# Turning the last 64 rows of four tiles apart, with their twin columns partly on GpSimd and the first copy on VectorE

## The chip, the cores and the metric

The kernel runs on one NeuronCore of a Trainium2 chip (trn2). The metric is device time in microseconds (us) of one execution. The ratios below are the mean time of one kernel's fast runs over the mean of the other's fast runs of the same rounds, so they are not quite the ratios of the medians quoted beside them.

Names used throughout: TensorE is PE in the profile, its weight loads PEld, VectorE DVE, ScalarE ACT, GpSimd POOL.

## The reference, cut to what matters

```python
xn = layernorm(x)                       # x: 2048 tokens x 448
s  = linear_attention(xn, wqkv, wo)     # q, k, v = xn @ wqkv; 16 heads of 28
h  = relu(xn @ w1 + b1) ** 2            # 448 -> 1792
g  = silu(h @ w2 + b2)
return x + s * g
```

The products with `wqkv` and `w1` take `xn` transposed, channels on partitions. 448 channels are three chunks of 128 and a rest of 64. A matmul over the rest has 64 rows (`64*128` in the profile, where a full chunk has `128*128`), and the kernel runs such matmuls in pairs, one on rows 0 to 63 and one on rows 64 to 127. In the kernel before the first pair, of 512 columns each, starts at 8.366 and 8.370 us and the next pair at 8.592: two of them in 0.226 us, where one matmul of 128 rows and 512 columns steps by 0.216. For the pairs the kernel keeps the last 64 channels on partitions 0 to 63 and again on 64 to 127: they are written twice before the transpose ("twin columns").

## The kernel before: the opening

The tokens are 16 tiles of 128. Tiles 4 to 15 are transposed by DMA, much later. Tiles 0 to 3, the opening, are transposed by TensorE into PSUM and copied to `xT`. The kernel lists operations by engine; a list scheduler orders VectorE, ScalarE and GpSimd, with a fixed order in the opening. TensorE's instructions stay in the order of the program.

```python
# (cut) statistics on VectorE, rstd = exp(-0.5*ln(var+eps)) on ScalarE, then on VectorE:
#   ln_norm: xn[:, si, 0:256], xn[:, si, 256:384] (tiles 0, 1) or xn[:, si, 0:384] (tiles 2, 3)
def ln_last(si):     # last 64 columns and their twins in one instruction
    x = x_tok[:, si, 384:448]
    x = bass.AP(tensor=x.tensor, offset=x.offset, ap=[x.ap[0], [0, 2], x.ap[1]])
    return add("dve", lambda e, _: e.tensor_scalar(
        out=xn[:, si, 384:512].rearrange("p (i c) -> p i c", i=2), in0=x, scalar1=mv[:, si, 0:1],
        scalar2=rstd[:, si : si + 1], op0=ALU.subtract, op1=ALU.mult), ...)

def pe_transpose(si, part, eng):   # transposes of one bank, then one copy to xT
    b = Buf("T")
    chunks = range(4) if part is None else (2 * part, 2 * part + 1)
    # (cut) one e.transpose for each chunk; a copy on `eng` of all chunks
    # (tile 0, part 0: two copies of one chunk each)

# rests(): the 64-row matmuls that complete a unit, two units at once
# phase((a, ks), (c, ks)): unit a on rows 0-63 beside unit c on rows 64-127
# pe_four(a, b, c, d): phase((a,K4),(c,K4)); phase((b,K4),(d,K4)); phase((c,K3),(a,K3)); phase((d,K3),(b,K3))
#   with K4 = (3, 0, 1, 2), K3 = (0, 1, 2): the rest (chunk 3) comes first
warm(8, wide=True)                 # 8 dummy matmuls of 512 columns
turn(0, 0, "act"); turn(0, 1, "act"); turn(1, 0, "act")
mains(k0, (0,)); mains(k0, (1,)); mains(k0, (2,))       # K of tile 0, 512 columns each
turn(1, 1, "act")
mains(k1, (0, 1)); h_mains(0, (0, 1)); mains(k1, (2,))  # K of tile 1; H of tiles 0 and 1
# (cut) transpose of b1
h_mains(0, (2,)); h_mains(1); h_mains(2)
head["xT2"] = pe_transpose(2, None, "act")
h_mains(3)
head["xT3"] = pe_transpose(3, None, "dve")
rests(k0, k1); rests(first[0], first[2]); rests(first[1], first[3])
pe_four(*second)                   # H of tiles 2 and 3
```

I call the second group of K matmuls (`mains(k1, (0, 1))`) "the second K group" and the first phase of the last line "the tile 2/3 phase".

Of the kernel before, what the change touches and what calls it, by code (L numbers as in the profile page):

```python
# [9 lines left out]
P = 128  # L10
# [45 lines left out]
class Program:  # L56
# [8 lines left out]
    def add(self, eng, emit, reads=(), writes=(), dur=0.2, alts=(), nbytes=0):  # L65
        op = Op(eng, emit, reads, writes, dur, alts, nbytes)
        for t in op.reads:
            w = self.writer.get(t)
            if w is not None:
                op.raw.add(w)  # L70
            self.readers.setdefault(t, []).append(op)
        for t in op.writes:
            w = self.writer.get(t)
            if w is not None and w is not op:
                op.deps.add(w)
            for r in self.readers.get(t, ()):
                if r is not op:
                    op.deps.add(r)
            self.writer[t] = op
            self.readers[t] = [r for r in self.readers.get(t, ()) if r is op]  # L80
        op.raw.discard(op)
        op.deps |= op.raw
        for d in op.deps:
            d.succ.append(op)
        self.ops.append(op)
        return op
# [203 lines left out]
def bass_recurrent_scan__linear_attn_block__dense_activation_squared_relu__prompt_kernel(  # L290
# [4 lines left out]
    with ExitStack() as es:  # L295
        sb = lambda name, shape, dtype: es.enter_context(nc.sbuf_tensor(name, shape, dtype))
        bf, f32 = dt.bfloat16, dt.float32
        pr = Program()
        add = pr.add

        ident = sb("ident", [P, P], bf)
# [7 lines left out]
        xn = sb("xn", [P, NT, 512], bf)  # L309
        xT = sb("xT", [P, 4, S], bf)  # L310
# [8 lines left out]
        mv = sb("mv", [P, NT, 2], f32)  # L319
        vep = sb("vep", [P, NT], f32)  # L320
        rstd = sb("rstd", [P, NT], f32)
# [23 lines left out]
        ps = lambda b: pbank[b.bank]  # L345
# [94 lines left out]
        wnames = lambda name: [(name, i) for i in range(4 if name == "w1a" else 3)]  # L440
# [53 lines left out]
            )  # L494

        xn_of = lambda si: [("xn", si, 0), ("xn", si, 1)] if si < 2 else [("xn", si)]
        xT_of = lambda si: [("xT", si, j) for j in ("a", 0, 1)[si > 0 :]] if si < 4 else [("xT", si)]

        def ln_twin(lo, hi, eng="dve"):

# [7 lines left out]
        def ln_last(si):  # L508

            x = x_tok[:, si, 384:448]  # L510
            x = bass.AP(tensor=x.tensor, offset=x.offset, ap=[x.ap[0], [0, 2], x.ap[1]])
            return add(
                "dve",
                lambda e, _: e.tensor_scalar(
                    out=xn[:, si, 384:512].rearrange("p (i c) -> p i c", i=2), in0=x, scalar1=mv[:, si, 0:1],
                    scalar2=rstd[:, si : si + 1], op0=ALU.subtract, op1=ALU.mult,
                ),
                [("x", si), ("mv", si), ("rstd", si)], [("xd", si)], 0.18,
            )

        def pe_transpose(si, part, eng):


            b = Buf("T")
            chunks = range(4) if part is None else (2 * part, 2 * part + 1)
            for i, c in enumerate(chunks):
                reads = xn_of(si)[c // 2 :][:1] or xn_of(si) if c < 3 else [("xd", si)]
                add(
                    "pe",
                    lambda e, _, i=i, c=c: e.transpose(  # L530
                        ps(b)[:, i * 64 : (i + 1) * 64].bitcast(bf), xn[:, si, c * P : (c + 1) * P], ident[:, :]
                    ),
                    reads + ["ident"] + ([b] if i else []), [b], 0.1,
                )
            def ev(e, _, lo=0, n=len(chunks)):
                src = ps(b)[:, lo * 64 : (lo + n) * 64].bitcast(bf).rearrange("p (c k) -> p c k", c=n)
                dst = xT[:, chunks[0] + lo : chunks[0] + lo + n, si * P : (si + 1) * P]
                if eng == "dve":
                    return e.tensor_copy(dst, src)
                return e.activation(out=dst, in_=src, func=AF.Copy)  # L540

            names = [("xT", si, j) for j in ((0, 1) if part is None else (part,))]
            if (si, part) == (0, 0):
                head["xT00a"] = add(eng, lambda e, x: ev(e, x, 0, 1), [b], [("xT", 0, "a")], 0.25)
                return add(eng, lambda e, x: ev(e, x, 1, 1), [b], names, 0.25)
            return add(eng, ev, [b], names, (0.42 if eng == "dve" else 0.6) if part is None else 0.25 if eng == "dve" else 0.35)

        def dma_transpose(si):
            op = add(
# [10 lines left out]
        def phase(lo, hi):  # L560


            todo = []
            order = [(i / len(ks), h, u, k) for h, (u, ks) in enumerate((lo, hi)) for i, k in enumerate(ks)]
            for _i, h, u, k in sorted(order, key=lambda o: o[:2]):
                todo.append((u, h, k, u.count == 0, u.count == u.steps - 1))
                u.count += 1

            def f(e, _):
                last = None  # L570
                for u, h, k, start, stop in todo:
                    last = u.mm(e, h, k, start, stop)
                return last

            reads, us = [], [u for u, ks in (lo, hi) if ks]
            for u in us:
                reads += [r for r in u.reads if r not in reads]
            dur = max(len(ks) * MM(u.n) for u, ks in (lo, hi) if ks)
            op = add("pe", f, reads + [u.bank for u in us if u.op], [u.bank for u in us], dur)
            for h, (u, ks) in enumerate((lo, hi)):  # L580
                if ks:
                    if u.op and u.half != h:
                        op.sync.add(u.op)
                    u.op, u.half = op, h
            for u in us[::-1]:
                if u.count == u.steps:
                    u.out()

        K4, K3 = (3, 0, 1, 2), (0, 1, 2)

        def pe_four(a, b, c, d):

            phase((a, K4), (c, K4))
            phase((b, K4), (d, K4))
            phase((c, K3), (a, K3))
            phase((d, K3), (b, K3))

        def mains(u, ks=K3, reads=None):


            def f(e, _):
                for k in ks:
                    last = u.mm(e, 2, k, k == 0, False)
                return last

            reads = u.reads if reads is None else reads
            add("pe", f, reads + ([u.bank] if ks[0] else []), [u.bank], len(ks) * MM(u.n))
# [440 lines left out]
        head = {}  # L1048
# [21 lines left out]
        k0, k1 = kk(0), kk(1)  # L1070
        first = [hh(0, fi, 0) for fi in range(4)]
        second = [hh(0, fi, 1, first[fi].bank) for fi in range(4)]

        def turn(si, part, eng):
            head[f"xT{si}{part}"] = pe_transpose(si, part, eng)

        def h_mains(fi, ks=K3):
            xs = xT_of(0) + xT_of(1)
            mains(first[fi], ks, [x for x in xs if 2 in ks or x[2] != 1] + [("w1a", fi // 2 * 3)])

        turn(0, 0, "act")
        turn(0, 1, "act")
        turn(1, 0, "act")
        mains(k0, (0,), [("xT", 0, "a")] + wnames("wk")[:1])
        mains(k0, (1,), [("xT", 0, 0)])
        mains(k0, (2,), [("xT", 0, 1)])
        turn(1, 1, "act")
        mains(k1, (0, 1), [("xT", 1, 0)] + wnames("wk")[:1])
        h_mains(0, (0, 1))
        mains(k1, (2,), [("xT", 1, 1)])  # L1090
        bb = Buf("B1")
        b1v = lambda: ps(bb)[:, 0 : P // 2].bitcast(bf)
        add("pe", lambda e, _: e.transpose(b1v(), b1r[:, :], ident[:, :]), ["b1r", "ident"], [bb], 0.1)
# [1 line left out]
            "act", lambda e, _: e.activation(out=b1f[:, :], in_=b1v()[:, 0:NF], func=AF.Copy), [bb], ["b1f"], 0.2  # L1095
        )
        h_mains(0, (2,))
        h_mains(1)
        h_mains(2)
        head["xT2"] = pe_transpose(2, None, "act")  # L1100
        h_mains(3)
        head["xT3"] = pe_transpose(3, None, "dve")
        n = len(pr.ops)
        rests(k0, k1)
        k0.out()
# [2 lines left out]
        rests(first[0], first[2])  # L1108
        rests(first[1], first[3])
        for eng, names in (  # L1110
            ("dve", "st0 mv0 st1 mv1 xn00 xn01 xd0 xn10 xn11 xd1 st2 mv2 st3 mv3 xd2 xn2 xd3 xn3 xT3"),
            ("act", "ln0 ex0 ln1 ex1 xT00a xT00 xT01 xT10 xT11 ln2 ex2 ln3 ex3 b1 xT2"),
        ):
            ops = [head[n] for n in names.split()]
            for i, op in enumerate(ops):
                op.after = ops[:i]
                op.prio = -100 + i
        for op in early:
            op.after = [head["xT3" if op.eng == "dve" else "xT2"]]
        pe_four(*second)  # L1120

        def quads(g, what):

# [15 lines left out]
        for g, (first, second) in enumerate(streams):  # L1139
            if g + 1 < NG:  # L1140
                n = len(pr.ops)
# [106 lines left out]
```

## Time and profile before

| what | before |
|---|---|
| time, median of 3 | 141.26 us (141.19 to 141.45) |
| TensorE busy | 136.5 of 139.5 us (98%) |
| first transpose | 4.190 us |
| first K matmul | 5.030 us |
| second K group | 5.789 us |
| tile 2/3 phase | 8.954 us |

The page of the kernel before, its engine line and the head of its chain that ended last:

```profile
PE 136.5 (98%) x1255; PEld 68.0 (49%) x1255; DVE 92.2 (66%) x226; ACT 78.0 (56%) x152; POOL 25.0 (18%) x33
...
PE 95%; DVE 2%; DMA 2%; issue 0%; DVEq 0%
```

TensorE bounds the kernel. The next view of the kernel before is the busy time by stretch: us in the stretch, then busy us of each engine.

```profile
core 0: us, PE busy (x) PEld busy (x) DVE busy (x) ACT busy (x) POOL busy (x), PEclk, DMA share, GB/s
...
9.00:74.00 65.00, 65.00 (x624) 30.26 (x626) 56.39 (x144) 55.00 (x106) 7.08 (x5) 1.00 0.47 102
```

From 9 to 74 us TensorE is never idle. The opening is where it waits. Busy time hides this, because a matmul's recorded end overlaps the next start (the first K matmuls of the kernel before are recorded with 0.379 us each and start 0.216 us apart); the weight loads show it better. The timeline of the kernel before, PEld alone (start, length, what; in brackets the idle time before it and who ended it):

```profile
4.19 0.54 PEld L530 LDWEIGHTS pb<-ident,xn 128*128 128x128 bf16 x4 [1.19 <-DVE xn L488]
4.90 0.11 PEld L530 LDWEIGHTS pb<-ident,xn 128*128 128x128 bf16 x2 [0.17 <-DVE xn L488]
4.98 0.15 PEld L643 LDWEIGHTS pb<-w_qkv,xT 128*128 128x128 bf16 x2
...
5.74 0.15 PEld L643 LDWEIGHTS pb<-w_qkv,xT 128*128 128x128 bf16 x2
...
8.03 0.23 PEld L530 LDWEIGHTS pb<-ident,xn 128*128 128x128 bf16 x4
8.36 0.10 PEld L643 LDWEIGHTS pb<-w_qkv,xT 64*128 64x128 bf16 x2
...
8.95 0.22 PEld L690 LDWEIGHTS pb<-xT,w 64*128 64x128 bf16 x6 [0.26 <-DVE xT L539]
```

Two waits: the first K matmul (weights at 4.98) stands behind tile 1's transposes (4.90), and the tile 2/3 phase at 8.95 waits for VectorE's copy of tile 3. I took each gap from the starts of single matmuls in the trace: 0.50 us in all before the first K matmul, about 0.10 at 8.366, where 64-row matmuls begin, and 0.142 at 8.954. VectorE in the same stretch, kernel before:

```profile
4.27 0.31 DVE L514 TENSOR_SCALAR xn<-x_tok,mv,rstd 128x128 bf16<-128x128 bf16 x1
4.50 0.57 DVE L488 TENSOR_SCALAR xn<-x_tok,mv,rstd 128x256 bf16<-128x256 bf16 x2
4.99 0.31 DVE L514 TENSOR_SCALAR xn<-x_tok,mv,rstd 128x128 bf16<-128x128 bf16 x1
5.21 0.62 DVE L465 BATCH_NORM_STATS2 st<-x_tok 128x6 f32<-128x448 bf16 x1
...
8.47 0.42 DVE L539 COPY xT<-pb 128x512 bf16<-128x512 bf16 x1 [0.49 <-PE pb L530]
```

Two twin pieces (L514) stand ahead of tile 2's statistics (5.21).

### The profile page before, as it was taken

What the parts mean: (1) busy time and instruction counts of PE and PEld (TensorE: products, weight loads), DVE (VectorE), ACT (ScalarE), POOL (GpSimd) and SP (SyncE); (2) the same over time, 40 slices, a digit from 0 to 9 for tenths busy, and PEclk for the clock granted to TensorE, in tenths of its full rate; (3) what the DMA queues carried; (4) which work ended last, traced back from release to release, by engine and by line L of the source; (5) the groups of instructions that cost most, each with busy time, mean ns of one, the idle gap of its engine ahead of it and who ended that gap; (6) DMA issues with size and microseconds to landing.
All of it is one profiled execution on the core that took longest, in us unless ns stands there. A gap on an engine that the chain in (4) does not pass through costs nothing.

```text
span 139.5 us, 3098 instructions
## 1 busy us (share of the span) xinstructions
PE 136.5 (98%) x1255; PEld 68.0 (49%) x1255; DVE 92.2 (66%) x226; ACT 78.0 (56%) x152; POOL 25.0 (18%) x33
## 2 busy tenths in 40 slices
PE   9999999999999999999999999999999999999993
PEld 2474444444444444444455455645555555555482
DVE  3989899798878995889995900219836072452743
ACT  4769787879988878979788912512033030300220
POOL 6000000000000000000893000000001429092670
PEclk9999999999999999999999999999999999999999
DMA  6996578999823300000000148970000103112132
GB/s 202 244 338 199 82 172 181 359 276 140 140 52 61 62 13 0 0 19 5 0 0 0 36 116 179 164 116 2 0 0 5 66 0 100 37 62 69 36 100 66
DMA packets 20353, 12.90 MB, mean 92 GB/s; under 512 B 9524, under 2 KB 19956, under 8 KB 20340
## 3 DMA queue, kind: packets, MB, share of 16 engines
q1 hardware_dynamic: 18332, 11.52, 34.5%
q10 hardware_dynamic: 2008, 1.20, 4.6%
q8 instruction: 10, 0.16, 0.5%
q14 instruction: 3, 0.02, 0.1%
HBM read 8.78 MB, written 2.10 MB: 78 GB/s over the span
## 4 chain that ended last, share of the span: by engine, by line
PE 95%; DVE 2%; DMA 2%; issue 0%; DVEq 0%
PE pb L957 31%; PE pb L690 30%; PE pb L643 9%; PE pb L1023 8%; PE pb L724 7%; PE pb L674 7%; DMA x_tok<-in_A_x_dram 2%; PE pb L530 1%; PE pb L730 1%; DVE st L465 1%; PE pb L817 1%; PE pb L778 1%; PE pb L855 0%; DVE xn L993 0%; DVE mv L466 0%; PE pb L848 0%
## 5 line engine op out<-in xcount | busy, mean ns | idle before, releaser
L690 PE MATMUL pb<-xT,w 64*128 64x512 bf16 (+2 forms) x408 | 51.6, 365 | 0.0
L957 PE MATMUL pb<-w,r 64*128 64x448 bf16 (+3 forms) x406 | 44.9, 343 | 0.0
L699 ACT ACTIVATE r<-pb,b1f 128x512 bf16<-128x512 f32 x56 | 35.2, 689 | 4.1 <-PE pb L690 4.1
L690 PEld LDWEIGHTS pb<-xT,w 64*128 64x128 bf16 (+1 forms) x408 | 22.8, 94 | 22.5 <-ACT r L699 0.5
L957 PEld LDWEIGHTS pb<-w,r 64*128 64x128 bf16 (+1 forms) x406 | 22.8, 95 | 19.9 <-issue 0.7
L933 ACT ACTIVATE gbuf<-gbuf 128x448 bf16<-128x448 bf16 (+1 forms) x16 | 8.7, 567 | 36.0 <-DVE gbuf L968 35.4
L968 DVE TENSOR_TENSOR gbuf<-pb,b2b 128x448 bf16<-128x448 f32 (+1 forms) x16 | 9.2, 608 | 29.5 <-PE pb L957 29.5
L1002 POOL TENSOR_TENSOR xn<-xn,x_tok 128x448 bf16<-128x448 bf16 x15 | 15.1, 1033 | 46.3 <-DVE xn L993 46.3
L643 PE MATMUL pb<-w_qkv,xT 64*128 64x512 bf16 (+1 forms) x106 | 17.8, 376 | 0.0
L674 PE MATMUL pb<-xT,w_qkv 64*128 64x512 bf16 x84 | 15.5, 376 | 0.0
L707 DVE TENSOR_TENSOR r<-r 128x512 bf16<-128x512 bf16 x42 | 14.4, 420 | 0.0
L392 POOL MEMSET kvm<- 128x2048 bf16 x1 | 1.8, 1806 | 63.5 <-DVE zb L668 63.5
L1023 PE MATMUL pb<-msb,pqT 64*128 64x448 bf16 (+3 forms) x93 | 10.9, 343 | 0.0
L631 DVE SCALAR_TENSOR_TENSOR qk<-pb,qk 128x512 bf16<-128x512 f32 x16 | 10.6, 685 | 0.2
L465 DVE BATCH_NORM_STATS2 st<-x_tok 128x6 f32<-128x448 bf16 x16 | 9.3, 609 | 2.1 <-DMA x_tok<-in_A_x_dram 2.1
L993 DVE TENSOR_TENSOR xn<-pb,gbuf 128x448 bf16<-128x448 f32 (+2 forms) x17 | 9.2, 591 | 2.0 <-ACT gbuf L933 1.5
L621 ACT ACTIVATE qk<-pb 128x512 bf16<-128x512 f32 x16 | 8.9, 595 | 2.9 <-PE pb L643 2.4
L643 PEld LDWEIGHTS pb<-w_qkv,xT 64*128 64x128 bf16 (+1 forms) x106 | 6.6, 94 | 6.0 <-ACT xT L540 0.2
L724 PE MATMUL pb<-qk,xn 128*128 128x448 bf16 x48 | 9.3, 353 | 0.0
L621 ACT ACTIVATE pqT<-pb 128x512 bf16<-128x512 f32 x12 | 6.8, 598 | 3.1 <-PE pb L690 1.5
L674 PEld LDWEIGHTS pb<-xT,w_qkv 64*128 64x128 bf16 x84 | 6.0, 94 | 5.0
L708 ACT ACTIVATE r<-r 128x512 bf16<-128x512 bf16 x14 | 8.4, 638 | 0.0
(71 smaller groups left out, 99.9 us busy)
## 6 DMA issues: line engine op xcount, KB each, us to landing
out_dram<-xn SPq DMA_DIRECT2D x15, 112.0 KB, 1.7
w<-in_B_w_dram SPq DMA_DIRECT2D x1, 1568.0 KB, 10.2
x_tok<-in_A_x_dram SPq DMA_DIRECT2D x3, 448.0 KB, 3.8
xT<-rows ACTq DMA_DIRECT2D x6, 112.0 KB
w<-in_B_w_dram SPq DMA_DIRECT2D x1, 576.0 KB, 5.7
xT<-rows SPq DMA_DIRECT2D x5, 112.0 KB
w_o<-in_A_wo_dram SPq DMA_DIRECT2D x1, 392.0 KB, 11.4
w_qkv<-in_A_wqkv_dram SPq DMA_DIRECT2D x1, 384.0 KB, 3.4
```

The lines of the kernel that those rows point to most:

```text
L465: add("dve", lambda e, _: e.bn_stats(st6[:, si, :], x_tok[:, si, :]), [("x", si)], [("st", si)], 0.58),
L621: add("act", lambda e, _: e.activation(out=slot, in_=src(), func=AF.Exp), [buf, "actw"], [tile], 0.6)
L631: lambda e, _: e.scalar_tensor_tensor(out=slot, in0=src(), scalar=1.0 + 1e-6, in1=slot, op0=ALU.add, op1=ALU.max),
L643: return e.matmul(ps(b)[:, 0:512], xT[half[h], c, si * P : (si + 1) * P], w_qkv[half[h], c, 384 : 2 * D], start=start, stop=stop,)
L674: return e.matmul(ps(b)[:, 0:512], w_qkv[half[h], c, m * P : (m + 1) * P], xT[half[h], c, g * 512 : (g + 1) * 512], start=start, stop=stop,)
L690: return e.matmul(ps(b)[:, c0 : c0 + n], w_1[half[h], c, fi * P : (fi + 1) * P], xT[half[h], c, t : t + n], start=start, stop=stop,)
L699: lambda e, _: e.activation(out=slot, in_=ps(b)[:, 0:512], func=AF.Relu, bias=b1f[:, fi : fi + 1]),
L707: return e.tensor_tensor(out=slot, in0=slot, in1=slot, op=ALU.mult)
L724: last = e.matmul(ps(b)[:, 0:D], xn[:, si, c * P : (c + 1) * P], pk_of(si), start=(si == 0), stop=(si == NT - 1),)
L957: return e.matmul(ps(b)[:, 0:n], r2[half[h], fi, si * P : (si + 1) * P], w_2[half[h], fi, c], start=start, stop=stop)
L1002: eng, lambda e, _: e.tensor_tensor(out=ob, in0=ob, in1=x_tok[:, si, c], op=ALU.add),
L1023: return e.matmul(ps(b)[:, 0:n], q, m, start=start, stop=stop)
```

## The change

The intent is to keep the rests off the critical path. Rests are needed late (in `rests` and at the end of the tile 2/3 phases), so their transposes and copies are taken out of the four tiles' first copies and done two tiles at a time. The twin columns of tiles 0 and 1 go to GpSimd. The first chunk is copied by VectorE, so that the first K matmul can start without waiting for a pair of transposes. The diff, cut to its core:

```diff
             return add(
-                "dve",
+                "pool" if si < 2 else "dve",
                 lambda e, _: e.tensor_scalar(            # ln_last: the twin columns
...
-        turn(0, 0, "act")
-        turn(0, 1, "act")
-        turn(1, 0, "act")
-        mains(k0, (0,), [("xT", 0, "a")] + wnames("wk")[:1])
-        mains(k0, (1,), [("xT", 0, 0)])
-        mains(k0, (2,), [("xT", 0, 1)])
-        turn(1, 1, "act")
+        turn("xT00", 0, (0,), "dve")          # name, first tile, chunks, copying engine, tiles
+        turn("xT01", 0, (1,), "act")
+        turn("xT02", 0, (2,), "act")
+        mains(k0, (0,), [("xT", 0, 0)] + wk0)
+        turn("xT10", 1, (0, 1), "act")
+        mains(k0, (1,), [("xT", 0, 1)])
+        turn("xT12", 1, (2,), "act")
+        mains(k0, (2,), [("xT", 0, 2)])
...
         h_mains(0, (2,))
+        turn("xT03", 0, (3,), "act", 2)
         h_mains(1)
+        turn("xT2", 2, K3, "act")
         h_mains(2)
-        head["xT2"] = pe_transpose(2, None, "act")
+        turn("xT3", 3, K3, "dve")
         h_mains(3)
-        head["xT3"] = pe_transpose(3, None, "dve")
+        turn("xT23", 2, (3,), "act", 2)
...
-            ("dve", "st0 mv0 st1 mv1 xn00 xn01 xd0 xn10 xn11 xd1 st2 mv2 st3 mv3 xd2 xn2 xd3 xn3 xT3"),
-            ("act", "ln0 ex0 ln1 ex1 xT00a xT00 xT01 xT10 xT11 ln2 ex2 ln3 ex3 b1 xT2"),
+            ("dve", "st0 mv0 st1 mv1 xn00 xn01 xT00 xn10 xn11 st2 mv2 st3 mv3 xn2 xd2 xn3 xd3 xT3"),
+            ("act", "ln0 ex0 ln1 ex1 xT01 xT02 xT10 xT12 ln2 ex2 ln3 ex3 b1 xT03 xT2 xT23"),
+            ("pool", "xd0 xd1"),
...
-        pe_four(*second)
+        phase((a, K3), (c, K3))               # without the rests of tiles 2 and 3
+        phase((a, (3,)), (c, (3,)))
+        phase((b, K4), (d, K4))
+        phase((c, K3), (a, K3))
+        phase((d, K3), (b, K3))
```

More of the change, by code (lines that the diff above doesn't have):

```diff
@@ L496, in bass_recurrent_scan__linear_attn_block__dense_activation_squared_relu__prompt_kernel @@
         xn_of = lambda si: [("xn", si, 0), ("xn", si, 1)] if si < 2 else [("xn", si)]
-        xT_of = lambda si: [("xT", si, j) for j in ("a", 0, 1)[si > 0 :]] if si < 4 else [("xT", si)]
+        xT_of = lambda si: [("xT", si, c) for c in range(4)] if si < 4 else [("xT", si)]
         def ln_twin(lo, hi, eng="dve"):
@@ L517, in ln_last, with turn, ev @@
                 ),
-                [("x", si), ("mv", si), ("rstd", si)], [("xd", si)], 0.18,
+                [("x", si), ("mv", si), ("rstd", si)], [("xd", si)], 0.87 if si < 2 else 0.22,
             )
-        def pe_transpose(si, part, eng):
+        def turn(name, si, chunks, eng, tiles=1):
             b = Buf("T")
-            chunks = range(4) if part is None else (2 * part, 2 * part + 1)
-            for i, c in enumerate(chunks):
-                reads = xn_of(si)[c // 2 :][:1] or xn_of(si) if c < 3 else [("xd", si)]
+            pieces = [(si + t, c) for t in range(tiles) for c in chunks]
+            n = len(pieces)
+            for i, (t, c) in enumerate(pieces):
+                reads = xn_of(t)[c // 2 :][:1] or xn_of(t) if c < 3 else [("xd", t)]
                 add(
                     "pe",
-                    lambda e, _, i=i, c=c: e.transpose(
-                        ps(b)[:, i * 64 : (i + 1) * 64].bitcast(bf), xn[:, si, c * P : (c + 1) * P], ident[:, :]
+                    lambda e, _, i=i, t=t, c=c: e.transpose(
+                        ps(b)[:, i * 64 : (i + 1) * 64].bitcast(bf), xn[:, t, c * P : (c + 1) * P], ident[:, :]
                     ),
-                    reads + ["ident"] + ([b] if i else []), [b], 0.1,
+                    reads + ["ident"] + ([b] if i else []), [b], 0.06,
                 )
-            def ev(e, _, lo=0, n=len(chunks)):
-                src = ps(b)[:, lo * 64 : (lo + n) * 64].bitcast(bf).rearrange("p (c k) -> p c k", c=n)
-                dst = xT[:, chunks[0] + lo : chunks[0] + lo + n, si * P : (si + 1) * P]
+            def ev(e, _):
+                src = ps(b)[:, 0 : n * 64].bitcast(bf)
+                dst = xT[:, chunks[0], si * P : (si + tiles) * P]
+                if len(chunks) > 1:
+                    src = src.rearrange("p (c k) -> p c k", c=n)
+                    dst = xT[:, chunks[0] : chunks[0] + n, si * P : (si + 1) * P]
                 if eng == "dve":
@@ L540, in ev @@
                 return e.activation(out=dst, in_=src, func=AF.Copy)
-            names = [("xT", si, j) for j in ((0, 1) if part is None else (part,))]
-            if (si, part) == (0, 0):
-                head["xT00a"] = add(eng, lambda e, x: ev(e, x, 0, 1), [b], [("xT", 0, "a")], 0.25)
-                return add(eng, lambda e, x: ev(e, x, 1, 1), [b], names, 0.25)
-            return add(eng, ev, [b], names, (0.42 if eng == "dve" else 0.6) if part is None else 0.25 if eng == "dve" else 0.35)
+            dur = 0.06 + 0.09 * n if eng == "dve" else 0.16 + 0.11 * n
+            head[name] = add(eng, ev, [b], [("xT", t, c) for t, c in pieces], dur)
         def dma_transpose(si):
@@ L1072, in bass_recurrent_scan__linear_attn_block__dense_activation_squared_relu__prompt_kernel @@
         second = [hh(0, fi, 1, first[fi].bank) for fi in range(4)]
-        def turn(si, part, eng):
-            head[f"xT{si}{part}"] = pe_transpose(si, part, eng)
         def h_mains(fi, ks=K3):
             xs = xT_of(0) + xT_of(1)
-            mains(first[fi], ks, [x for x in xs if 2 in ks or x[2] != 1] + [("w1a", fi // 2 * 3)])
-        turn(0, 0, "act")
-        turn(0, 1, "act")
-        turn(1, 0, "act")
-        mains(k0, (0,), [("xT", 0, "a")] + wnames("wk")[:1])
-        mains(k0, (1,), [("xT", 0, 0)])
-        mains(k0, (2,), [("xT", 0, 1)])
-        turn(1, 1, "act")
-        mains(k1, (0, 1), [("xT", 1, 0)] + wnames("wk")[:1])
+            mains(first[fi], ks, [x for x in xs if x[2] in ks] + [("w1a", fi // 2 * 3)])
+        wk0 = wnames("wk")[:1]
+        turn("xT00", 0, (0,), "dve")
[6 more added lines that the diff above has]
+        mains(k0, (2,), [("xT", 0, 2)])
+        mains(k1, (0, 1), [("xT", 1, 0)] + wk0)
         h_mains(0, (0, 1))
-        mains(k1, (2,), [("xT", 1, 1)])
+        mains(k1, (2,), [("xT", 1, 2)])
         bb = Buf("B1")
@@ L1118, in bass_recurrent_scan__linear_attn_block__dense_activation_squared_relu__prompt_kernel @@
         for op in early:
-            op.after = [head["xT3" if op.eng == "dve" else "xT2"]]
-        pe_four(*second)
+            op.after = [head["xT3" if op.eng == "dve" else "xT23"]]
+        a, b, c, d = second
+        full_reads = [(u, u.reads) for u in (a, c)]
+        for u, r in full_reads:
+            u.reads = [n for n in r if isinstance(n, Buf) or n[0] != "xT" or n[2] < 3]
+        phase((a, K3), (c, K3))
+        for u, r in full_reads:
+            u.reads = r
+        phase((a, (3,)), (c, (3,)))
+        phase((b, K4), (d, K4))
+        phase((c, K3), (a, K3))
+        phase((d, K3), (b, K3))
         def quads(g, what):
```

## The prediction

> **What bounds the kernel.** TensorE. The page has PE busy 136.5 of 139.5 us (98%) and PE 95% of the chain that ended last. From the starts of single matmuls in the trace I took each gap beyond the streaming time (512 columns step by 0.216 us, 256 by 0.109, a transpose by 0.056). After 9 us the gaps come to about 1.1 us in all, nearly all after 74 us, which the change does not touch. So only the opening can pay, and each 0.1 us saved there should arrive at the end.
>
> **The opening now.** First transpose at 4.19 us, set by the first normalised piece on VectorE (3.82). From there to the first two-row-group phase over tiles 2 and 3 (8.954) PE has about 4.0 us of work and 0.76 us idle: 0.50 before the first K matmul (5.030, which stands in PE's order behind tile 1's first two transposes at 4.907 and 4.974), 0.012 at 7.486, 0.098 at 8.366 on going from 128-row to 64-row matmuls (the same gap stands at 94.18 and 130.04, so it stays; the weights had landed by 6.9), and 0.142 at 8.954, waiting for VectorE's copy of tile 3 (8.472, 0.425 us). This 0.76 us (0.5% of the time) is a ceiling.
>
> **What the change does.** Transposes and matmuls keep their number and shapes. Tile 0's first chunk is copied by VectorE: transpose ends 4.42, copy starts 4.46 and lasts about 0.22 us (estimate: 512 columns took 0.425), so the first K matmul comes near 4.78 instead of 5.03. The two twin pieces leave VectorE (0.223 us of its order each), the copy enters. Tile 1's normalisation then starts near 4.6 instead of 4.503; its transposes at 5.0 to 5.1, ScalarE's 256-column copy (0.385) from 5.3 to 5.7, so the second K matmul group starts at 5.8 to 5.9, against 5.789 before, with two transposes fewer done (0.11 us of work still owed). The early start is thus spent again on that wait. The real gain is at the end of the opening: tiles 2 and 3 no longer wait for their last rows, tile 3's copy shrinks and comes about 0.3 us earlier, and the 0.142 us wait goes. Net: 0.142 + 0.012 saved, 0.1 to 0.2 lost.
>
> **GpSimd.** Its two normalisations read and write SBUF while VectorE runs the critical ones. [...] a mask instruction on GpSimd that takes 0.3 us elsewhere lasted 4.46 us (68.785 to 73.24), until the run of 13 squares on VectorE had ended (73.09). So I expect GpSimd's first piece to be stretched to 0.7 to 0.9 us, running in VectorE's gap at 4.36, and delaying tile 1's normalisation to about 4.7. [...] Its results are needed near 6.8: ample.
>
> **Prediction.** 141.2 us, range 140.9 to 141.6; faster by over 2%: 1%; within 2%: 98%; slower: 1%.
>
> **Signs.** Right: first K matmul near 4.8; the second K group still at 5.75 to 5.95 behind ScalarE's copy; GpSimd pieces of 0.7 to 0.9 us; the tile 2/3 phase at 8.85 to 9.05 with no wait; PE gap-free from there to 74 us. Wrong: first transpose later than 4.2, or new PE gaps after 9 us.
>
> **What could make it wrong.** [...] a different order of evictions on ScalarE and VectorE downstream (the order is chosen by a list scheduler) that starves PE of banks; ScalarE's later phi of tile 0, behind one more copy.

The forecast's sum for the opening was 0.154 us saved (0.142 + 0.012) against 0.1 to 0.2 lost, so between 0.05 us gained and 0.05 lost. That GpSimd's pieces would be stretched rests on the one mask instruction in the trace alone; their 0.7 to 0.9 us was the author's estimate.

## The result

| | before | after |
|---|---|---|
| time, median (6 runs each, same rounds) | 141.35 us (141.18 to 141.66) | 141.21 us (141.13 to 141.41) |
| ratio of fast runs | | 0.999, 95% interval 0.9975 to 1.0005 |
| profiled span | 139.5 us | 139.6 us |
| first transpose | 4.190 | 4.187 |
| first K matmul | 5.030 | 4.794 |
| second K group | 5.789 | 5.919 |
| tile 2/3 phase | 8.954 | 9.043 |

The times do not tell the two apart (the interval of the ratio includes 1). The timeline of the changed kernel, PEld, against that of before:

```profile
4.18 0.38 PEld L531 LDWEIGHTS pb<-ident,xn 128*128 128x128 bf16 x3 [1.19 <-DVE xn L488]
4.79 0.10 PEld L645 LDWEIGHTS pb<-w_qkv,xT 128*128 128x128 bf16 x1 [0.22 <-DVE xT L544]
...
5.92 0.11 PEld L645 LDWEIGHTS pb<-w_qkv,xT 128*128 128x128 bf16 x2 [0.32 <-ACT xT L545]
...
8.59 0.10 PEld L645 LDWEIGHTS pb<-w_qkv,xT 64*128 64x128 bf16 x2
8.61 0.53 PEld L692 LDWEIGHTS pb<-xT,w 64*128 64x128 bf16 x8
```

The first K matmul is 0.236 us earlier, but the second K group (5.92) now waits for ScalarE's copy. The wait for tile 3's copy is gone: at 8.61 the loads run on. GpSimd and VectorE of the changed kernel:

```profile
3.84 1.74 POOL L514 TENSOR_SCALAR xn<-x_tok,mv,rstd 128x128 bf16<-128x128 bf16 x2 [2.63 <-ACT rstd L479]
```

```profile
4.51 0.22 DVE L544 COPY xT<-pb 128x128 bf16<-128x128 bf16 x1
4.65 0.61 DVE L488 TENSOR_SCALAR xn<-x_tok,mv,rstd 128x256 bf16<-128x256 bf16 x2
5.19 0.61 DVE L465 BATCH_NORM_STATS2 st<-x_tok 128x6 f32<-128x448 bf16 x1
...
8.26 0.36 DVE L544 COPY xT<-pb 128x384 bf16<-128x384 bf16 x1 [0.28 <-PE pb L531]
```

The two twin pieces left VectorE, yet tile 2's statistics start at 5.19 against 5.21. The place was filled by the copy and by a wait for it. (At full clock, in run 5 below, they start 0.07 us earlier: 0.959 us after the first transpose against 1.034.)

From 9 to 74 us the changed kernel has no idle TensorE either:

```profile
9.00:74.00 65.00, 65.00 (x626) 30.30 (x624) 56.38 (x144) 55.33 (x106) 7.01 (x5) 1.00 0.44 102
```

So what stands at 9 us stands at the end. The traces show it directly: from the start of the tile 2/3 phase to the end of the span it is 130.58 us in both kernels, 130.58 to 130.59 in four of the five other profiles below without a hold, and 130.67 in the fifth (`again`). The spans of these seven profiles, 139.50 to 140.09 us, thus differ almost only by when that phase starts. This profile even says "0.09 us later". But it has an oddity, seen in the TensorE timelines. The kernel before, then the changed one:

```profile
5.03 0.81 PE L643 MATMUL pb<-w_qkv,xT 128*128 128x512 bf16 x3
```

```profile
4.79 0.54 PE L645 MATMUL pb<-w_qkv,xT 128*128 128x512 bf16 x1
```

Three K matmuls took 0.81 us from first start to last end before (0.379 us each, overlapping); a single one took 0.54 after. Its transposes took 0.288 us in place of 0.230. By these lengths the opening of the changed kernel ran at a lower TensorE clock; its trace has no record of the clock. Was that the change, or chance?

### The profile page after: what moved, and what is told of

Same layout as the page of the kernel before. It is cut to its first block, busy times and chain, and to the rows that moved or that the text cites. A ratio compares the mean times of both kernels' runs of the same rounds, so it can differ in the third digit from the quotient of the medians.

```text
span 139.6 us, 3096 instructions
## 1 busy us (share of the span) xinstructions
PE 136.6 (98%) x1255; PEld 68.4 (49%) x1255; DVE 92.3 (66%) x225; ACT 78.3 (56%) x153; POOL 26.8 (19%) x35
## 4 chain that ended last, share of the span: by engine, by line
PE 95%; DVE 2%; DMA 2%; issue 0%; DVEq 0%
PE pb L959 31%; PE pb L692 30%; PE pb L645 9%; PE pb L1025 8%; PE pb L726 7%; PE pb L676 6%; DMA x_tok<-in_A_x_dram 2%; PE pb L732 1%; PE pb L531 1%; DVE st L465 1%; PE pb L819 1%; PE pb L780 1%; PE pb L857 0%; DVE xn L995 0%; DVE mv L466 0%; PE pb L850 0%
```

## Experiments

Twelve more runs were made. All gave the right result. "Full clock" below means that the first transpose took 229 to 231 ns, "half clock" that it took 286 to 289. The names go by the clock where it is on record: in the kernel before, full clock is on record from 4.05 us on; matmuls of 512 columns and 128 rows step by 0.216 us after that, and the dummy ones ahead of it, after the first, by 0.427 (634 ns each). In the one stretch with 0.50 on record (run 10) two K matmuls that stand alone took 0.61 and 0.63 us. Because the first transpose itself moves by up to 0.08 us between profiles (it comes 1.86 us after the first statistics on VectorE, which wait for `x`, in all seven profiles without a hold), positions are given from its start.

### 1. The changed kernel once more (`again`)

No edit.

> The changed kernel, not edited. In its first profile the opening's matmuls ran at half speed until about 5.1 us (first K matmul 538 ns, against 379 in the kernel before; its start to the next step 0.374 against 0.216), and the second K group came at 5.919. My theory: when the TensorE clock rises is a matter of chance in each execution, not of the change. Then a second profile may show 219 to 230 ns transposes and a 379 ns first K matmul, with the second K group at 5.75 to 5.85 and the first tile 2/3 phase near 8.9. Rival: the change itself (GpSimd at work, or the other order) slows the first matmuls; then 288 ns transposes, a 538 ns first K matmul and 5.92 come again. Time in both: 0.998 to 1.000 of the kernel before.

Measured: 141.36 us against 141.6 (0.9986, interval 0.9964 to 1.0008). The first transpose took 286 ns again and the first K matmul 457 ns; the second K group came 1.650 us after the first transpose (1.732 in the first profile), the tile 2/3 phase at 4.789 (4.856). Half clock again, but for a shorter time, so the length of that stretch is not fixed by the code. Two profiles in a row at half clock left the rival alive; the next runs decided it.

### 2. The second half alone (`tail_only`)

On the kernel before, only tiles 2 and 3 are handled as in the change:

```diff
         h_mains(1)
+        turn("xT2", 2, K3, "act")
         h_mains(2)
-        head["xT2"] = pe_transpose(2, None, "act")
+        turn("xT3", 3, K3, "dve")
         h_mains(3)
-        head["xT3"] = pe_transpose(3, None, "dve")
+        turn("xT23", 2, (3,), "act", 2)
 ...     # and the tile 2/3 phases, and the order xn2 xd2 xn3 xd3, as in the change
```

> The kernel before with only the second half of the change: tiles 2 and 3 without their last rows first (copies of 384 columns), last rows of both turned together, and the first tile 2/3 phase without them. Tiles 0 and 1, twins and first copy as before. My theory: this holds the whole gain. The wait of 0.142 us ahead of the first tile 2/3 phase goes, so that phase starts at about 8.81 (if the clock has risen by 4.2; later by up to 0.2 if not) and the time is 0.999 of the kernel before, PE gap-free to 74 us. Rival: the copy of the last rows only moves the wait; then a new gap of about 0.1 us at the step that needs them, near 9.0 to 9.1, and 1.000.

Measured: 141.53 us against 141.6 (1.0011, interval 0.998 to 1.0042). The profile ran at half clock until about 6.0 us (first K matmul 634 ns; the second to the third step is 0.427 us, the third to the next 0.226), with the tile 2/3 phase at 5.237. Here GpSimd had no twins, and TensorE's order was that of the kernel before until well after the clock rose. So half clock comes without the change too. As a test of the second half the run was spoiled; run 6 repeats it.

### 3. The first half alone (`head_only`)

The changed kernel with tiles 2 and 3 put back:

```diff
         h_mains(1)
-        turn("xT2", 2, K3, "act")
         h_mains(2)
-        turn("xT3", 3, K3, "dve")
+        turn("xT2", 2, range(4), "act")
         h_mains(3)
-        turn("xT23", 2, (3,), "act", 2)
+        turn("xT3", 3, range(4), "dve")
 ...     # order xd2 xn2 xd3 xn3 and pe_four(*second) as before
```

> The changed kernel with tiles 2 and 3 turned, copied and multiplied as in the kernel before; tiles 0 and 1, GpSimd twins and VectorE's first copy as changed. My theory: the first half of the change gains nothing and loses about 0.1 us, since the second K group still waits for ScalarE's copy (at 5.8 with an early clock, 5.9 with a late one) with two transposes fewer behind it. First tile 2/3 phase at 9.0 to 9.15, with a wait of 0.05 to 0.15 us ahead of it; time 1.000 to 1.001. Rival: the early first K matmul (4.79) is worth its 0.2 us to the end; then that phase starts by 8.85 and the time is 0.9985.

Measured: 141.51 us against 141.6 (1.0001, interval 0.9978 to 1.0023). This profile had full clock, with twins on GpSimd: the first transpose took 229 ns, the first K matmul 389. First K matmul 0.550 after the first transpose (0.840 before), second K group 1.581 (1.599 before), tile 2/3 phase 4.846 with a wait of 0.141 ahead of it. Against 4.764 in the kernel before, the first half alone loses 0.08 us, as expected: the 0.29 us at the first K matmul is spent by the second K group, and two transposes (0.112 us) are still owed.

### 4. Two copies for tile 1's first two chunks (`split_copy`)

```diff
-        turn("xT10", 1, (0, 1), "act")
+        turn("xT10", 1, (0,), "act")
+        turn("xT11", 1, (1,), "act")
-        mains(k1, (0, 1), [("xT", 1, 0)] + wk0)
+        mains(k1, (0,), [("xT", 1, 0)] + wk0)
+        mains(k1, (1,), [("xT", 1, 1)])
```

> The changed kernel, but tile 1's first two chunks go to two banks with two 128-column ScalarE copies in place of one of 256 columns (0.384 us), and the second K group's two matmuls wait for one each. If that copy is what holds the second K group, its first matmul comes 0.10 to 0.16 us earlier (5.65 with an early clock, 5.8 with a late one), the first tile 2/3 phase moves as much, and the time is 0.998 to 0.999 of the kernel before. If something else holds it (the semaphores, the clock), it stays at 5.79 or 5.92.

Measured: 141.56 us against 141.6 (1.000, interval 0.998 to 1.002); half clock until about 5.8 us (estimated from a step of 0.374 us at 5.455, which is 0.427 at half and 0.216 at full clock), second K group at 1.867. Spoiled like run 2.

### The hold: taking the clock out

Of the six profiles so far, two had full clock in the opening (the kernel before and `head_only`). The trace's clock records say that the clock rose at 4.05 us and 3.96 us there; the five half-clock profiles among the runs without a hold (`again`, `tail_only`, `split_copy`, the changed kernel, and later `split_late3`) carry no clock record at all, so a mean clock of 1.0 on their pages (`again` shows 1.000, with a first transpose of 286 ns) means nothing for the opening. In the kernel before, the stretch of full clock on record lasts 136.53 us from 4.05 on, past the end of the span. The latest rise of the six was the 6.0 us estimated for `tail_only`.

So I held the opening back in both kernels, to a first transpose at 10.5 us, with the same edit. That the clock would be full by then was my estimate from these moments; nothing so far showed when it has to rise:

```diff
+        for _j in range(4):     # on GpSimd, about 7.4 us; gates the first statistics
+            pool(lambda e, _: e.memset(kvm[:, :, :], 0.0), ["kvm", "delay"], ...)
-        add("dve", ... e.bn_stats(st6[:, si, :], x_tok[:, si, :]), [("x", si)], ...)
+        add("dve", ... e.bn_stats(...), [("x", si)] + (["delay"] if si == 0 else []), ...)
-        warm(8, wide=True)
+        warm(20, wide=True)
+        warm(7, wide=True, after=["delay"])
```

### 5. Both kernels held back (`w_before`, `w_after`)

> The kernel before, with the opening held back so that chance is taken out of the clock: four dummy fills on GpSimd (about 7.5 us) gate the first statistics on VectorE, TensorE runs 20 wide dummy matmuls meanwhile and 7 more after the fills. Results stay right; about 6 us are added. If the spread of the times and the shifts between profiles come from when the TensorE clock rises, all matmuls of the opening are at full speed here (transposes 219 to 230 ns), the six times of this kernel lie within 0.25 us (the plain kernel before: 141.1 to 143.18 on this chip's runs), and the first tile 2/3 phase starts 4.76 us after the first transpose with a wait of 0.14 us. Rival: the spread has another cause (DMA, the launch) and stays at 0.4 us or more.

> The changed kernel with the same held-back opening. My theory at full clock: second K group 1.58 us after the first transpose, behind ScalarE's 256-column copy; first tile 2/3 phase 4.70 us after the first transpose with no wait, so 0.06 us less than the kernel before held back likewise, and 0.00 to 0.10 us less in time. Rival (the early first K matmul pays in full): 4.5 us and 0.25 us less. Rival [...]: transposes above 280 ns again, 4.8 us or more, and no gain.

Both profiles had full clock (first transposes 230 and 231 ns). The second rival took slow transposes for a part of the change; they did not come. The weight loads, held-back kernel before, then held-back changed kernel:

```profile
10.55 0.57 PEld L532 LDWEIGHTS pb<-ident,xn 128*128 128x128 bf16 x4 [0.65 <-DVE xn L490]
...
15.33 0.22 PEld L692 LDWEIGHTS pb<-xT,w 64*128 64x128 bf16 x6 [0.26 <-DVE xT L541]
```

```profile
10.53 0.12 PEld L533 LDWEIGHTS pb<-ident,xn 128*128 128x128 bf16 x2 [0.63 <-DVE xn L490]
...
12.11 0.11 PEld L647 LDWEIGHTS pb<-w_qkv,xT 128*128 128x128 bf16 x2 [0.32 <-ACT xT L547]
...
14.85 0.64 PEld L694 LDWEIGHTS pb<-xT,w 64*128 64x128 bf16 x10
```

From single matmul starts, after the first transpose: second K group 1.609 before, 1.579 after; tile 2/3 phase 4.773 before (4.764 without the hold), 4.742 after. The wait for tile 3's copy (0.140) is there before and gone after. At full clock the change is worth 0.03 us, about half of the 0.06 expected. That is one profile of each; two profiles of the kernel before at full clock differ by 0.01. The same code that gave 4.856 in its first profile gives 4.742 here, and tile 3's copy comes 0.33 us earlier than in the held-back kernel before (3.963 against 4.292), as predicted.

The expectation on spread failed: the held-back kernel before took 148.03 to 148.76 us in the 4 runs on record, all with a recorded mean clock of 1.0, the changed one 147.76 to 148.9 in 6. Of these six, the two longest (148.81 and 148.9) have a mean clock of 0.988, estimated from run 10 to be one stretch of 3.41 us at half clock (that run has one such stretch on record, and the same mean); the other four lie within 0.26 us. So in the changed kernel the clock goes with the spread; in the kernel before the recorded clock does not explain it. The hold also shifts the schedule later on, and TensorE then has gaps at 44 to 46 us (0.84 us in the held-back kernel before, whose waits name DMA transposes and ScalarE; 0.40 us in the changed one) which the plain kernels do not have. So the times of held-back kernels say nothing about the opening, and I use only their traces up to the tile 2/3 phase. In the seven profiles without a hold the differences arise ahead of the tile 2/3 phase (see the result); how much of the spread of the unprofiled runs is the clock stays open.

### 6. The second half alone, held back (`w_tail_only`)

> The kernel before with only the tile 2/3 half of the change, held back likewise. Without the hold its profile ran at half clock until about 6.2 us and told nothing. My theory: first tile 2/3 phase 4.62 us after the first transpose, 0.14 less than the held-back kernel before and 0.08 less than the held-back changed kernel; time 0.1 to 0.2 us less than the held-back kernel before. Rival (both halves are worth the same, or the first half is the one that pays): 4.70 or more, time as the held-back kernel before.

Measured: full clock, tile 2/3 phase at 4.786. My theory (4.62) fell; the rival stands. The wait for tile 3's copy is gone, but the transposes of tiles 2 and 3, now one H group earlier, wait 0.11 and 0.05 us for their normalised rows. From the first transpose, tile 2's normalisation starts 0.21 us later than in `w_after` (2.639 against 2.433). Two engines delay it. ScalarE and VectorE of this kernel, then of `w_after`:

```profile
12.36 0.38 ACT L542 ACTIVATE xT<-pb 128x256 bf16<-128x256 bf16 x1 [0.38 <-PE pb L532]
12.64 0.28 ACT L477 ACTIVATE vep<-mv,eps 128x1 f32<-128x1 f32 x1
13.20 0.38 DVE L490 TENSOR_SCALAR xn<-x_tok,mv,rstd 128x384 bf16<-128x384 bf16 x1
```

```profile
12.36 0.29 ACT L477 ACTIVATE vep<-mv,eps 128x1 f32<-128x1 f32 x1
12.97 0.35 DVE L490 TENSOR_SCALAR xn<-x_tok,mv,rstd 128x384 bf16<-128x384 bf16 x1
```

VectorE still carries the twins of tiles 0 and 1, so tile 2's variance (`mv`) is ready 0.08 us later. But ScalarE's ln for it (`vep`) starts 0.26 us later: it stands behind ScalarE's copy of tile 1's second pair of chunks, which in the changed kernel is a copy of one chunk and already done. VectorE's order thus explains 0.08 us of the 0.21; the rest is ScalarE's order. The held-back kernel before shows the same copy ahead of the same ln.

### 7. The split copy, held back (`w_split_copy`)

> The changed kernel with tile 1's first two chunks in two copies, held back likewise. Without the hold the clock rose only at about 5.9 us. My theory: ScalarE's 256-column copy is what holds the second K group; halved, the group starts 1.42 to 1.48 us after the first transpose in place of 1.58, the first tile 2/3 phase at 4.55 to 4.60, and the time is 0.1 to 0.2 us less than that of the held-back changed kernel. Rival: the group waits for something else; 1.58 and 4.70 as in the held-back changed kernel.

Measured: second K group at 1.429, 0.15 us earlier, as expected: ScalarE's 256-column copy does hold it. But the tile 2/3 phase came at 4.739, not 4.55 to 4.60. The weight loads of this kernel show where the 0.15 us went:

```profile
13.55 0.26 PEld L694 LDWEIGHTS pb<-xT,w 128*128 128x128 bf16 x3
14.12 0.17 PEld L533 LDWEIGHTS pb<-ident,xn 128*128 128x128 bf16 x3 [0.30 <-DVE xn L490]
```

Tile 3's transposes wait for tile 3's normalisation on VectorE, a gap of 0.19 us by starts. In `w_after` the same transposes start at the same 14.12 with a gap of 0.03 us. VectorE's chain (statistics of tiles 2 and 3, ScalarE's ln and exp, normalisation) sets that moment in both.

### 8. The twins back on VectorE (`w_twins_dve`)

```diff
-                "pool" if si < 2 else "dve",
+                "dve",
-            ("dve", "... xn10 xn11 st2 ...
+            ("dve", "... xn10 xn11 xd0 xd1 st2 ...
```

> The held-back changed kernel with the twin pieces of tiles 0 and 1 back on VectorE, after tile 1's normalisation. Theory formed from the last runs (tiles 2 and 3 wait for VectorE's chain of statistics and normalisation, so what GpSimd takes off that chain is what pays): the statistics of tile 2 start 0.35 to 0.40 us later, the transposes of tile 3 wait for their normalised rows by 0.3 to 0.4 us, and the first tile 2/3 phase is at 5.05 to 5.15 us after the first transpose against 4.742. Rival (the twin pieces are off the critical path either way): 4.70 to 4.80.

This run and the next two held-back ones (9 and 10) ran once each, for the profile; their times say nothing. Measured, full clock: tile 2's statistics 1.331 us after the first transpose against 0.959, gaps of 0.17 and 0.21 us ahead of the transposes of tiles 2 and 3, tile 2/3 phase at 5.091 (4.742 in `w_after`). The delay and the position are as expected; the wait of 0.3 to 0.4 us expected ahead of tile 3 came in two parts. What GpSimd takes off VectorE is worth 0.35 us in the changed order.

### 9. The twins later on GpSimd (`w_twins_late`)

```diff
-                [("x", si), ("mv", si), ("rstd", si)], [("xd", si)], 0.87 if si < 2 else 0.22,
+                [("x", si), ("mv", si), ("rstd", si)] + ([("st", 2)] if si < 2 else []), [("xd", si)], ...
```

> The held-back changed kernel, same order on every engine, but GpSimd's two twin pieces also wait for tile 2's first statistics, so they run while VectorE is in statistics and no longer beside its normalisations (mask instructions ran beside such statistics at their usual 0.21 to 0.31 us). [...] here it takes 0.3 to 0.45 us, the normalisations of tile 1 on VectorE shrink from 0.353 and 0.355 us to 0.33 and 0.30 as in the kernel before, tile 2's statistics start 0.05 to 0.08 us earlier, and the first tile 2/3 phase is at 4.68 to 4.74 us after the first transpose. Rival (0.85 us is simply what GpSimd needs for this): 0.85 us again, the second piece ends near 13.9, the last-row transposes of tiles 0 and 1 wait some 0.7 us, and that phase comes at 5.3 or later.

The theory was that VectorE's company makes up most of a twin piece's 0.83 to 0.88 us.

The groups of GpSimd in the first 16 us, the changed kernel, then this one:

```profile
L514 POOL TENSOR_SCALAR xn<-x_tok,mv,rstd 128x128 bf16<-128x128 bf16 x2 | 1.7, 875 | 2.6 <-ACT rstd L479 2.6
```

```profile
L516 POOL TENSOR_SCALAR xn<-x_tok,mv,rstd 128x128 bf16<-128x128 bf16 x2 | 1.7, 852 | 3.5 <-DVE st L467 3.5
```

A mean of 852 ns against 875: the mean hides that the second piece, beside VectorE's normalisation of tile 2, took 0.905 us. The first piece took 0.800 us with almost nothing but statistics beside it on VectorE (12.16 to 12.96). The theory of its length fell: nearly alone this instruction took 0.800 us on GpSimd, and beside the normalisation 0.1 us more. The last-row transposes then waited 0.695 us and the tile 2/3 phase came at 5.388, as the rival said. What did show is the other direction, VectorE slowed while GpSimd works. Here the second and fourth normalising pieces of tiles 0 and 1 took 0.310 and 0.305 us, against 0.364 and 0.355 in `w_after` (without the hold 0.309 and 0.307 in the kernel before, 0.360 each in the changed one, where they end 0.31 and 0.30 us before the GpSimd piece beside them), and tile 3's normalisation, now beside GpSimd, took longer. VectorE, this kernel:

```profile
13.60 0.54 DVE L490 TENSOR_SCALAR xn<-x_tok,mv,rstd 128x384 bf16<-128x384 bf16 x1
```

It was 0.41 in `w_after`. Tile 2's statistics began 0.07 us sooner here (0.887 after the first transpose, 0.959 in `w_after`). That is the price of the two engines side by side in the changed kernel.

### 10. Split copy, and tile 3 turned later (`w_split_late3`, `split_late3`)

On `split_copy`:

```diff
-        turn("xT3", 3, K3, "dve")
         h_mains(3)
+        turn("xT3", 3, K3, "dve")
```

> The held-back changed kernel with tile 1's copy split in two, and tile 3's transposes put behind the fourth H group in place of ahead of it. In the split kernel the 0.15 us won at the second K group were lost again in a wait of 0.19 us for tile 3's normalised rows. Theory: with that wait moved behind 0.33 us of matmuls it goes, and the first tile 2/3 phase starts 4.53 to 4.60 us after the first transpose (4.739 in the split kernel, 4.773 in the kernel before). Rival: tile 3's copy on VectorE then comes too late and the phase waits for it; 4.70 or more with a gap ahead of it.

The held-back run had bad luck with the clock. Its stretches, with the granted clock as the third number from the right:

```profile
3.22:6.63 3.41, 3.04 (x14) 1.19 (x12) 0.00 (x0) 0.00 (x0) 3.35 (x2) 1.00 1.00 271
6.63:10.05 3.42, 1.34 (x7) 0.61 (x7) 1.32 (x3) 0.46 (x2) 1.96 (x2) 1.00 0.96 326
10.05:13.46 3.41, 3.37 (x13) 1.37 (x12) 3.05 (x11) 2.29 (x11) 2.95 (x7) 0.50 0.83 237
```

TensorE was busy only 1.34 us of the second window, and for the whole third one the clock was halved: the first 2.9 us from the first transpose, out of 5.7 to the tile 2/3 phase. Why is not shown: in `w_before` TensorE was busy 1.35 us of the same second window, and the third had a clock of 1.00. The tile 2/3 phase came at 5.662; inconclusive.

> The same version without the held-back opening: what it is worth in time. Theory: 0.2 us less than the kernel before when the clock rises early, up to 0.4 us of chance either way in a single run; ratio 0.998 to 0.9995, not to be told from 1 by five rounds with certainty. Rival: 1.000 or more.

Measured: 141.08 us against 141.47 in the same rounds, 0.9984, interval 0.9965 to 1.0002: better in the median by 0.39 us, not clear of noise. The profile was at half clock at first (first transpose 288 ns, first K matmul 547), much like the changed kernel's first profile (288 and 538). From the step after the first K matmul (0.383 and 0.374 us) I estimate that the clock rose 0.95 and 0.93 us after the first transpose. The weight loads show no wait after 5.78 us, where the second K group waits 0.16 us for ScalarE's copy, and from single starts the second K group is at 1.590 (1.732 in that profile) and the tile 2/3 phase at 4.702 (4.856). Two profiles of like clock thus differ by 0.15 us in favour of this version. That it beats the kernel before in time is not shown, and it never ran in the same rounds as the changed kernel.

## Why the prediction was right

The time was 141.21 us, for 141.2 predicted. That the number agrees to 0.01 us is luck: the same code took 141.36 us in the next rounds (`again`), and the medians of the kernel before range from 141.25 to 141.6. What the prediction got right by reasoning is that the change is worth next to nothing, because a wait won at one place is spent at another. Point by point:

- **Only the opening can pay, 0.76 us at most.** Right: from the tile 2/3 phase to 74 us the starts of single matmuls show no gap over 0.03 us in either kernel, and from that phase to the end both take 130.58 us.
- **First K matmul near 4.78.** Right: 4.794, but at half clock; at full clock it came 0.550 us after the first transpose, 4.74 on the same scale.
- **Second K group at 5.8 to 5.9, the early start spent.** Right: 5.919, waiting for ScalarE's copy; at full clock 1.579 after the first transpose, 5.77 on the same scale. Shortening that copy moved the group by 0.15 us (run 7).
- **0.142 us saved at the tile 2/3 phase, 0.1 to 0.2 lost.** Right: the wait is gone, and at full clock the rests begin 0.11 us later (4.297 after the first transpose, 4.187 in the held-back kernel before). Net 0.03 us.
- **GpSimd's pieces of 0.7 to 0.9 us.** The number was right (0.881 and 0.869), the reason wrong. The prediction had them "stretched", after a mask instruction that took 4.46 us beside VectorE's squares and 0.30 after them (68.785 and 73.311 us in the kernel before). With the normalisations taken away the first piece still took 0.80 us (run 9), so company made up 0.1 us at most. It cost VectorE 0.07 us at tile 2's statistics.
- **Where the real gain lies.** The prediction, and after it my expectation for the second half alone, put it in tiles 2 and 3. Run 6 refuted that: alone, the first half loses 0.08 us and the second gains nothing (0.01 us later, no more than two profiles of one kernel differ). The second half pays only with the first, which brings tile 2 sooner to its normalisation in two ways: GpSimd takes the twins off VectorE (run 8), and tile 1's last chunk is copied earlier, so that ScalarE's ln does not wait behind it (run 6). Run 8 shows the first of these by an edit; the second is read from traces. The twins alone on GpSimd, with the first copy left to ScalarE, were never run.
- **What it missed.** The clock. A chance of 0.05 to 0.45 us in one execution (`again` at 4.789, the same code held back at 4.742; `tail_only` at 5.237, held back at 4.786) is larger than the whole effect, and it made the first profile of the changed kernel look slower.

At full clock, tile 2/3 phase after the first transpose:

| kernel | us |
|---|---|
| before (held back: 4.773) | 4.764 |
| first half alone, not held back | 4.846 |
| second half alone, held back | 4.786 |
| changed, held back | 4.742 |
| changed, split copy, held back | 4.739 |
| changed, twins on VectorE, held back | 5.091 |
| changed, twins late on GpSimd, held back | 5.388 |

## What to carry to other kernels

In an opening where several engines hand tiles to TensorE, removing one wait mostly uncovers the next: find the chain that sets the last hand-over (here statistics and normalisation of tiles 2 and 3 on VectorE, with ScalarE's ln and exp between them) before shortening an earlier one. When two profiles differ by a few tenths of a microsecond near the start, compare the lengths of equal matmuls first, since the clock may differ (the first K matmul took 379 ns in the kernel before and 538 in the changed kernel's first profile), and measure positions from a common event. A predicted duration that comes true does not confirm its reason; moving the instruction to other company tests it.
